# The last four rows of w4: a load written as 8 groups of 16 partitions instead of 128 partitions

## Chip, core and metric

One core of one Trainium2 chip. The metric is device time in microseconds (us) of one execution, taken as the median of several. A "packet" below is one entry of the DMA records: the move of one contiguous row by one of the core's 16 DMA engines. A "completion" is one entry of a semaphore's record of landings. A load of the kernel before has sixteen, which I read as one an engine: those of the last load come 0.3 to 0.4 us after an engine's last packet (the last packet of all ends at 209.82, the last completion is at 210.21). Both are in the trace with their times. No record names the DMA engine, so an engine is followed by its packets: in the kernel before, 99% start 3 or 4 ns before the recorded end of the one before, the others at most 24 ns before and 10 ns after it.

## The reference

Attention over a sliding window of a KV cache plus a small MLP, at batch 4 with one new token. Only the last line of the MLP matters here.

```python
xn = layernorm(x)                                   # x: [4, 1, 576] bf16
# A: q = xn @ wq; scores over the last 2048 rows of k_cache (16 heads); softmax; @ v_cache; @ wo
# B: x1 = xn + hs; hs is zero for one token, as its shifts move every value out
h2 = gelu(layernorm(x1) @ w3) @ w4                  # w3 [576, 4608], w4 [4608, 576]
return x + A(xn) + x1 + h2
```

(So w1 and w2 do not matter, and the kernel leaves them out.)

## The kernel before

Nearly all the time is the loading of 87 MB: K and V of 16 heads at 2 MB each, wq, wo, w3 and w4. SP (SyncE) issues all loads, in one order, w4 last. w4 is loaded in five pieces, so that the matrix engine can use one while the next arrives; the last piece is four rows per partition, 128 x 4608 B.

```python
    W4_PIECES = [0, NFH // 2, NFH, NFH + 9, NFH + 14, NF]      # NFH = 18, NF = 36: ..., 9, 5 and 4 rows

    def load_w4():
        t = wp.tile([P, NF, D], BF16, tag="w", name="w4_sb")   # P = 128 partitions, D = 576
        for lo, hi in zip(W4_PIECES, W4_PIECES[1:]):
            e = lo // NFH
            src = B_w4[e * (F // 2):(e + 1) * (F // 2), :].rearrange("(p i) n -> p i n", i=NFH)
            nc.sync.dma_start(out=t[:, lo:hi, :], in_=src[:, lo - e * NFH:hi - e * NFH, :])
        w_tiles["w4"] = t
    # ...
    def acc_matmuls(lhsT, rhs):                                # 4 matmuls for each row of w4
        for i in range(NQD):
            nc.tensor.matmul(out=acc[i * QD:i * QD + B, :], lhsT=lhsT, rhs=rhs[:, i * CW:(i + 1) * CW],
                             start=False, stop=False, skip_group_check=True)

    def mlp_out(lo, hi):
        w4 = w_tiles["w4"]
        for i in range(lo, hi):
            acc_matmuls(gT[:, i, :], w4[:, i, :])
    # ... attention, w3, gelu -> gT ...
    pieces = list(zip(W4_PIECES, W4_PIECES[1:]))
    mlp_out(*pieces[0])
    o_spread(hl)
    o_pick(hl)
    mlp_out(*pieces[1])
    o_proj(hl)
    for lo, hi in pieces[2:]:
        mlp_out(lo, hi)

    fin = const.tile([P, CW], out.dtype)
    nc.vector.tensor_copy(out=fin[:], in_=acc[:])              # then four small output DMAs
```

## Time and profile before

| | before |
|---|---|
| median time | 216.23 us (216.14 to 216.32, 3 runs) |
| span of the profiled run | 214.6 us |
| PE busy | 121.0 us, 56% |
| loads (queue q1) | 87.17 MB, 95.7% of 16 engines' span |

From the page of the kernel before. The DMA row gives the mean busy share of the 16 DMA engines in tenths, in 40 equal slices of the span; the GB/s row is what they moved. The q lines give packets, MB and the share of 16 engines' span.

```profile
span 214.6 us, 6449 instructions
PE 121.0 (56%) x2893; PEld 94.9 (44%) x2893; DVE 118.0 (55%) x223; ACT 70.1 (33%) x258; POOL 6.1 (3%) x14
...
DMA  5999999999999999999999999999999999999960
GB/s 207 429 437 434 428 429 425 425 425 437 426 429 423 437 431 419 439 425 434 431 428 425 428 428 430 422 434 431 429 418 428 437 419 425 437 427 422 419 262 12
...
q1 hardware_dynamic: 7080, 87.17, 95.7%
q8 instruction: 22, 0.36, 0.6%
```

The DMA engines are busy from the second slice to the last but two, and no compute engine is over 56%. The kernel is bound by its loads. Without moving fewer bytes, the place to look for a gain is the last two slices, where the rate falls from 419 to 262 to 12 GB/s.

The end of the chain of waits of the kernel before, read downwards: when each step began, how long it took, what it was.

```profile
152.04 30.72 DMA kn<-in_A_k_cache_dram
182.76 0.02 issue
182.78 27.43 DMA w_sb<-in_B_w_dram
210.21 0.04 issue
210.26 0.68 PE acc L247 x16
210.93 0.02 issue
210.96 0.31 DVE fin L480
```

The load of w4's last piece lands at 210.21; its 16 matmuls and a cast follow at once. What moves 210.21 moves the time.

The timeline of the kernel before, the lines of the last three pieces of w4 (36, 20 and 16 matmuls) and the cast: start, length, and in brackets the idle time before and what ended it.

```profile
207.14 0.73 PE L247 MATMUL acc<-w_sb,gT 128*4 128x144 bf16 x36 [1.17 <-DMA w_sb<-in_B_w_dram]
208.88 0.77 PE L247 MATMUL acc<-w_sb,gT 128*4 128x144 bf16 x20 [1.00 <-DMA w_sb<-in_B_w_dram]
210.26 0.65 PE L247 MATMUL acc<-w_sb,gT 128*4 128x144 bf16 x16 [0.61 <-DMA w_sb<-in_B_w_dram]
210.96 0.31 DVE L480 CAST fin<-acc 128x144 bf16<-128x144 f32 x1 [5.87 <-PE acc L247]
```

PE waits before each.

The sixteen completions of the last piece in the trace:

```
205.50 205.62 205.65 205.70 205.73 205.77 206.55 207.32 | 208.64 208.78 208.83 209.74 209.96 210.07 210.15 210.21
```

Six engines are done by 205.77, two more by 207.32 (I put them down to the five 8 KB instruction fetches of another queue, q14: around those at 154.0 and 163.6 us two completions go from 0.51 and 0.95 us behind the first, at the load of 151.44, to 1.11 and 1.93, at that of 166.02), and eight come from 208.64 on. The packets say why. PE's instructions are fetched by DMA too, in 16 KB blocks (the 22 packets of q8). The blocks fall on eight of the sixteen engines in a fixed rotation: an engine that carries the first carries the ninth and the seventeenth. Around one such block an engine's packets read (start in ns, length, bytes, queue):

```
31906  611 16384 q1
32513  929 16384 q8     <- instruction fetch
33428 1107 16384 q1
34531  612 16384 q1
```

From there on the engine is 1.415 us behind, for good. The completions of the earlier loads show it step by step. Before the first fetch the sixteen lie within 0.56 us of each other. After the fetch that starts at 15.0 us one engine is 1.58 us behind the first; each further fetch puts one more behind, until eight are. Then the second round begins: the ninth fetch (107.8) leaves one engine 2.91 us behind, the seventeenth (168.5) one 4.49 us. Two or three fetches in 210 us make the late eight up to 4.7 us later than the early six. No engine catches up: the sixteen of the last piece still lie 4.71 us apart.

### The profile page before, as it was taken

To read this page: it belongs to the slowest core of one execution; us is meant where nothing else is said; L and a number is where in the kernel's file an instruction comes from. 1 tells how busy PE (TensorE), PEld (TensorE's weight loads), DVE (VectorE), ACT (ScalarE), POOL (GpSimd) and SP (SyncE) were. 2 spreads that over 40 slices of the span, in tenths; PEclk is the share of its full clock that TensorE was granted. 3 is DMA by queue.
4 is the path that set the end of the run, shared out by engine and by line. 5 is a ranking of instruction groups with operands and counts; after the bars stand their busy time and mean duration, and the time that the engine had idled before them with its cause. 6 is when DMAs were issued, how large, how long until landed. Compare 5 with 4: busy or idle time off the path is not lost. (4 is left out here: it accounts for less than half of the span.)

```text
span 214.6 us, 6449 instructions
## 1 busy us (share of the span) xinstructions
PE 121.0 (56%) x2893; PEld 94.9 (44%) x2893; DVE 118.0 (55%) x223; ACT 70.1 (33%) x258; POOL 6.1 (3%) x14
## 2 busy tenths in 40 slices
PE   0461355647470017157999577677474705779752
PEld 0350143445360015145899456555453604557641
DVE  5608799766470047348610798785573924854210
ACT  0000005571634001607070045570725340709600
POOL 5400100000000000000000000000000000000000
PEclk9999999999999999999999999999999999999995
DMA  5999999999999999999999999999999999999960
GB/s 207 429 437 434 428 429 425 425 425 437 426 429 423 437 431 419 439 425 434 431 428 425 428 428 430 422 434 431 429 418 428 437 419 425 437 427 422 419 262 12
DMA packets 7123, 87.58 MB, mean 408 GB/s; under 512 B 820, under 2 KB 824, under 8 KB 1336
## 3 DMA queue, kind: packets, MB, share of 16 engines
q1 hardware_dynamic: 7080, 87.17, 95.7%
q8 instruction: 22, 0.36, 0.6%
q14 instruction: 5, 0.04, 0.0%
q10 hardware_dynamic: 16, 0.00, 0.0%
HBM read 87.17 MB, written 0.00 MB: 406 GB/s over the span
## 5 line engine op out<-in xcount | busy, mean ns | idle before, releaser
L302 ACT ACTIVATE pt<-S 32x128 bf16<-32x128 f32 x256 | 68.5, 268 | 92.0 <-issue 55.3
L259 DVE STREAM_TRANSPOSE kt<-kn 128x1024 int32<-128x1024 int32 x64 | 74.3, 1205 | 11.4 <-DMA kn<-in_A_k_cache_dram 11.4
L313 PE MATMUL O<-pt,vn 128*128 128x8 bf16 x1024 | 37.4, 169 | 43.2 <-DMA vn<-in_A_v_cache_dram 41.7
L313 PEld LDWEIGHTS <-vn 128*128 128x128 bf16 x1024 | 34.4, 105 | 51.3 <-DMA vn<-in_A_v_cache_dram 43.6
L273 PE MATMUL S<-qz,kt 128*128 128x32 bf16 x1024 | 39.1, 189 | 25.2 <-DVE kt L259 25.2
L273 PEld LDWEIGHTS <-kt 128*128 128x128 bf16 x1024 | 33.6, 106 | 36.1 <-DVE kt L259 30.4
L287 DVE TENSOR_REDUCE m<-mxT 8x1 f32<-8x128 f32 x16 | 4.4, 277 | 42.6 <-PE mxT L285 42.6
L316 PE MATMUL O<-pt,ones_bf 128*128 128x64 bf16 x128 | 17.1, 226 | 0.0
L302 ACT ACT_TABLE_LOAD x1 | 1.3, 1283 | 32.6 <-DVE mx L280 32.6
L368 PEld LDWEIGHTS <-w_sb 128*128 128x128 bf16 x144 | 11.4, 164 | 0.5 <-issue 0.4
L368 PE MATMUL AB<-ln2T,w_sb 128*128 128x4 bf16 x144 | 11.5, 202 | 0.0
L280 DVE TENSOR_REDUCE mx<-S 128x8 f32<-128x512 f32 x16 | 10.4, 652 | 1.0 <-PE S L273 1.0
L295 PE MATMUL S<-dg,ones_bf 8*128 8x512 bf16 x16 | 9.6, 601 | 0.1
L265 PE MATMUL S<-negbig,ohT 4*128 4x512 bf16 x16 | 9.6, 601 | 0.0
L316 PEld LDWEIGHTS <-ones_bf 128*128 128x128 bf16 x128 | 8.4, 104 | 0.0
L370 PE MATMUL AB<-ln2T,w_sb 128*128 128x4 bf16 x36 | 7.3, 202 | 0.0
L247 PE MATMUL acc<-w_sb,gT 128*4 128x144 bf16 x144 | 4.8, 294 | 2.8 <-DMA w_sb<-in_B_w_dram 2.8
L324 DVE TENSOR_REDUCE dn<-O 128x8 f32<-128x64 f32 x16 | 3.3, 208 | 5.5 <-PE O L316 5.5
L375 DVE COPY g_x<-AB 128x144 f32<-128x144 f32 x1 | 0.3, 307 | 10.7 <-PE AB L370 10.7
L285 PE MATMUL mxT<-ident_f,mx 128*8 128x128 f32 x16 | 6.0, 374 | 0.3 <-DVE mx L280 0.3
L370 PEld LDWEIGHTS <-w_sb 128*128 128x128 bf16 x36 | 5.9, 165 | 0.0
L247 PEld LDWEIGHTS <-gT 128*4 128x4 bf16 x144 | 3.4, 104 | 3.6 <-issue 3.5
(72 smaller groups left out, 64.9 us busy)
## 6 DMA issues: line engine op xcount, KB each, us to landing
kn<-in_A_k_cache_dram SPq DMA_DIRECT2D x16, 2048.0 KB, 29.3
vn<-in_A_v_cache_dram SPq DMA_DIRECT2D x16, 2048.0 KB, 27.0
wo_sb<-in_A_wo_dram SPq DMA_DIRECT2D x4, 1152.0 KB, 28.8
w_sb<-in_B_w_dram SPq DMA_DIRECT2D x2, 2304.0 KB, 31.8
wq_sb<-in_A_wq_dram SPq DMA_DIRECT2D x4, 1024.0 KB, 4.9
w_sb<-in_B_w_dram SPq DMA_DIRECT2D x3, 1296.0 KB, 32.8
w_sb<-in_B_w_dram SPq DMA_DIRECT2D x2, 576.0 KB, 32.2
w_sb<-in_B_w_dram SPq DMA_DIRECT2D x1, 720.0 KB
```

The lines of the kernel that those rows point to most:

```text
L247: nc.tensor.matmul(out=acc[i * QD:i * QD + B, :], lhsT=lhsT, rhs=rhs[:, i * CW:(i + 1) * CW], start=False, stop=False, skip_group_check=True)
L259: nc.vector.transpose(out=kt[:], in_=src)
L265: nc.tensor.matmul(out=S_ps[h][:].rearrange("p g k j -> p (g k) j"), lhsT=ohT[:], rhs=nb, start=True, stop=False, skip_group_check=True)
L273: nc.tensor.matmul(out=S_ps[h][:, s * (SC // NQD) + g].rearrange("p k j -> p (k j)"), lhsT=kt[:, ib, g * NQD:(g + 1) * NQD, e:2 * QD:2].re ...
L280: nc.vector.reduce_max(out=mx[:], in_=S_ps[h][:].rearrange("p g k j -> p j (g k)"), axis=AX.X)
L285: nc.tensor.transpose(out=mxT[:], in_=st[h][:], identity=ident_f[:])
L295: nc.tensor.matmul(out=S_ps[h][:].rearrange("p g k j -> p (g k) j"), lhsT=ones_bf[0:NJ, :], rhs=dg, start=False, stop=False, skip_group_ch ...
L302: nc.scalar.activation(out=PT[h][kb * QD:(kb + 1) * QD, :, c4, :], in_=S_ps[h][c4 * QD:(c4 + 1) * QD, :, kb, :], func=ACT.Exp, scale=scale)
L313: nc.tensor.matmul(out=O_ps[h][:, 0:NJ], lhsT=vn[:, g * NQD + s, :], rhs=pt[:, g, s, :], start=(g == 0 and s == 0), stop=False, skip_group ...
L316: nc.tensor.matmul(out=O_ps[h][:, NJ:].rearrange("p (c j) -> p c j", j=NJ), lhsT=ones_bf[:], rhs=pt[:, g:g + DG, s, :], start=False, stop= ...
L368: nc.tensor.matmul(out=g_ps[:, i, :], lhsT=w3[:, j * F + e * (F // 2) + f0:j * F + (e + 1) * (F // 2):NFH], rhs=ln2T[:, j, :], start=False ...
L370: nc.tensor.matmul(out=g_ps[:, i, :], lhsT=w3[:, KJ * F + f0:KJ * F + F // 2:NFH], rhs=ln2T[:, KJ + e, :], start=False, stop=False, skip_g ...
```

## The change

The last piece keeps its bytes and its place in the queue. Its source is written as 8 groups of 16 partitions, so that, as I read its purpose, the transfer is split over 8 DMA engines with 16 packets each and no longer over 16 with 8 each. If those eight are the early ones, the late ones have nothing more to do for this piece and end sooner.

```diff
             src = B_w4[e * (F // 2):(e + 1) * (F // 2), :].rearrange("(p i) n -> p i n", i=NFH)
-            nc.sync.dma_start(out=t[:, lo:hi, :], in_=src[:, lo - e * NFH:hi - e * NFH, :])
+            src = src[:, lo - e * NFH:hi - e * NFH, :]
+            if hi == NF:
+                src = src.rearrange("(u p) i n -> u p (i n)", u=8)
+            nc.sync.dma_start(out=t[:, lo:hi, :].rearrange("p i n -> p (i n)") if hi == NF else t[:, lo:hi, :], in_=src)
```

## The prediction

> **What bounds it now.** The loads. In the 40-slice view the DMA row reads 9 from the second slice to the last but one; the SP queue moves 87.17 MB, 95.7% of 16 engines' span (queue table). The chain of waits ends with a DMA of w4 (27.43 us from 182.78), the last 16 matmuls at 210.26 and the cast at 210.96; the span ends at 214.6. PE waits for the last three w4 pieces (1.17, 1.00, 0.61 us in the timeline).
>
> The 16 engines do not end together. The sixteen completions of the last piece come at 205.50 to 205.76 (six), 206.55, 207.32, and then eight from 208.64 to 210.21. The packets of the trace, each starting as the one before it on its engine ends, show why: the 22 instruction fetches of 16 KB (queue q8) go in turn to eight of the engines, and each sets its engine back by 1.415 us.
>
> **What the change does.** Same bytes, same queue order, same compute instructions. The last piece (128 rows of 4608 B, 178 ns a packet) goes from 16 engines x 8 packets (1.40 us) to 8 engines x 16 packets (2.80 us). [...] No record of this run names an engine. [...]
>
> **Worth, three cases (estimates from those durations).**
> 1. Only the engines limit. The late eight end 1.40 us sooner (last completion 210.21 to 208.85); the early ones end at 206.6 to 208.4. PE then runs the last 20 and 16 matmuls (0.77 and 0.65 us) together after 208.9: 0.8 us saved, 215.4 us.
> 2. The SBUF side limits. [...] A packet here moves at 27.3 GB/s beyond a fixed 9 ns[...]. [...] the end stays near 210.2, or 0.5 us later [...]: 216.2 to 216.8 us.
> 3. The eight are the late ones: +1.4 us or more, 217.6 us and above.
>
> I weigh 2 highest, then 1, then 3.
>
> **Prediction: 216.2 us, 8 in 10 between 215.1 and 217.6. Faster by over 2%: 0.01; within 2%: 0.96; slower by over 2%: 0.03.**
>
> **What would show it.** The 4608 B packets of the last piece on eight engines, 16 each. Case 1: they stay at 178 ns, no wait or a short one between the last two w4 pieces, last matmul near 210.1. Case 2: they take 200 to 400 ns, and so do packets of the late engines at that time. Case 3: completions of the last piece come from late engines only, until 211.6 or later. Nothing before 203 us changes.
>
> **What would make it wrong.** Fetches falling elsewhere at the end; packets split differently[...].

The "8 engines x 16 packets" is my assumption, and so is case 1's, that the eight are early ones; the low weight of case 3 rested on it. The sums: 215.4 us in case 1; in case 2 the end stays near 210.2 (216.2 us) or comes 0.5 us later (216.8 at most); 217.6 us and above in case 3; together 216.2 us. The 27.3 GB/s and 9 ns of case 2 fit the usual packets of the kernel before: 4096 B in 159 ns, 4608 B in 178, 10368 B in 389, 16384 B in 611, 18432 B in 686.

## More of the kernel before

Unless said otherwise every run quoted is a fast one.

The windows view of the kernel before (stretch, its length, busy us and instruction counts of PE, PEld, DVE, ACT and POOL, granted PE clock, DMA share, GB/s):

```profile
204.00:206.00 2.00, 1.98 (x75) 1.57 (x72) 0.85 (x2) 0.00 (x0) 0.00 (x0) 1.00 0.85 354
206.00:208.00 2.00, 0.73 (x36) 0.58 (x36) 0.00 (x0) 0.00 (x0) 0.00 (x0) 1.00 0.54 224
208.00:210.00 2.00, 0.77 (x20) 0.56 (x20) 0.00 (x0) 0.00 (x0) 0.00 (x0) 0.69 0.29 116
```

From 206 to 210 us about half, then under a third, of the DMA engines work. They do not end together.

## The result, and the profile after

| | before | after |
|---|---|---|
| median time | 216.25 us (216.14 to 216.32, 4 runs) | 216.28 us (216.14 to 216.39, 4 runs) |
| ratio | | 1.0004, 95% interval 0.9989 to 1.0019 |
| span of the profiled run | 214.6 us | 214.6 us |
| last completion of w4 | 210.21 | 210.22 |
| completions of the last piece | 16 | 16 |
| its packets | 128 of 4608 B, 178 ns each | 128 of 4608 B, 178 ns each |

A ratio is the mean time of one kernel's fast runs over the mean of the other's in the same rounds, so it is not quite the ratio of the medians quoted. All outputs are right.

The page of the kernel after:

```profile
span 214.6 us, 6449 instructions
...
DMA  5999999999999999999999999999999999999960
...
q1 hardware_dynamic: 7080, 87.17, 95.7%
```

Its chain of waits, the end:

```profile
183.01 27.20 DMA w_sb<-in_B_w_dram
210.22 0.04 issue
210.26 0.68 PE acc L250 x16
...
210.96 0.31 DVE fin L483
```

Its timeline, the same four groups:

```profile
207.15 0.73 PE L250 MATMUL acc<-w_sb,gT 128*4 128x144 bf16 x36 [0.83 <-DMA w_sb<-in_B_w_dram]
208.89 0.49 PE L250 MATMUL acc<-w_sb,gT 128*4 128x144 bf16 x20 [1.01 <-DMA w_sb<-in_B_w_dram]
210.26 0.65 PE L250 MATMUL acc<-w_sb,gT 128*4 128x144 bf16 x16 [0.89 <-DMA w_sb<-in_B_w_dram]
210.96 0.31 DVE L483 CAST fin<-acc 128x144 bf16<-128x144 f32 x1 [5.82 <-PE acc L250]
```

And its windows:

```profile
206.00:208.00 2.00, 1.05 (x53) 0.69 (x42) 0.00 (x0) 0.00 (x0) 0.00 (x0) 1.00 0.55 224
208.00:210.00 2.00, 0.49 (x20) 0.33 (x20) 0.00 (x0) 0.00 (x0) 0.00 (x0) 0.85 0.26 105
```

The last 16 matmuls and the cast start at the same hundredth of a microsecond, and the DMA engines thin out in the same way. The sixteen completions, 205.44 to 210.22, show no trace of a split over eight engines.

The built program settles it: the DMA is the same one. A source written as 8 groups (16 partition rows apart) of 16 (one partition row apart) describes the same walk as 128 partitions one row apart. The builder folds the two dimensions into one, and in both kernels the instruction carries (step and count, in elements):

```
source       [10368 x 128] [1 x 2304]     offset 1335168
destination  [20736 x 128] [1 x 2304]     offset 18432
```

It carries 128 on both sides, and in both kernels the load has sixteen completions and 128 packets of 178 ns. That the two are one DMA was to be seen without a run: the listing of the built instructions names the transfer 128x2304 before and after. I had that listing and did not look at that line.

### The profile page after: what moved, and what is told of

Same layout as the page of the kernel before. It is cut to its first block, busy times and chain, and to the rows that moved or that the text cites. A ratio compares the mean times of both kernels' runs of the same rounds, so it can differ in the third digit from the quotient of the medians.

```text
span 214.6 us, 6449 instructions
## 1 busy us (share of the span) xinstructions
PE 120.9 (56%) x2893; PEld 95.0 (44%) x2893; DVE 118.1 (55%) x223; ACT 70.3 (33%) x258; POOL 6.2 (3%) x14
```

## The experiments

The kernel after answers nothing about eight engines, because it never used them. So the experiments first make the intended split real, then ask why it does what it does. A transfer whose dimensions cannot be folded must put the rows on other partitions, and so the matching rows of gT must be permuted (one matmul with a permutation matrix and two copies, before the loads end). Runs of one group shared a chip and its runs of the kernel before.

My first theory was the prediction's middle case: the writing into the on-chip memory limits, so that moving packets to other engines gains nothing. The rivals were its other two cases: only the engines limit (a gain), or the eight chosen are the late ones (a loss). Which partitions and engines would collide was my assumption, which no run here shows. Theory B below is that the writing limits as well, theory C that the engines used are the late ones.

### e0_perm_only: the permutation alone

```diff
         nc.vector.tensor_tensor(out=gT[:], in0=u[:], in1=xs[:], op=ALU.mult)
+        pm = const.tile([P, P], BF16, name="pm")
+        nc.vector.tensor_copy(out=pm[:], in_=ident_bf[:])        # here the identity
+        gp = ps_m.tile([P, 4, B], F32, tag="m", name="gp")
+        nc.tensor.matmul(out=gp[:].rearrange("p i b -> p (i b)"), lhsT=pm[:],
+                         rhs=gT[:, NF - 4:NF, :].rearrange("p i b -> p (i b)"), start=True, stop=True)
+        nc.vector.tensor_copy(out=gT[:, NF - 4:NF, :], in_=gp[:])
```

> Control: the load of before, plus the small extra step that the next three kernels need (a 128x128 permutation matrix, here the identity, one matmul and two copies after the gelu). Every theory expects the time of before, 216.25 us within 0.1%, the last w4 piece on 16 engines with 8 packets of 178 ns, last completion near 210.2 us.

Measured: 216.30 us against 216.37, ratio 0.9995 (0.9979 to 1.0012), last completion 210.15. The added work costs nothing, so what e1 to e3 show is the load's doing.

### e1_eight: the split over eight engines, made real

```diff
+            if hi == NF:
+                src = src.rearrange("(p u) i n -> u p (i n)", u=8)      # 8 x 16, row order changed
+                dst = dst.rearrange("p i n -> p (i n)")                 # dst was t[:, lo:hi, :]
     # cut: the DMA itself; pm as in e0, but it permutes gT's rows to match
```

The source is now [10368 x 8] [82944 x 16] [1 x 2304], which cannot be folded.

> The change made real: the row order of the last four rows is such that the two outer dimensions (8 and 16) cannot be merged into 128, so that eight engines carry 16 packets each. Theory A (the change as written was folded back into the same 128-row transfer, and only the engines limit): packets stay at 178 ns, all on the eight early engines, last completion 208.85 us, some 0.8 us faster, 215.4 us. Theory B [...]: about half of the 4608 B packets take 200 to 530 ns, last completion 210.2 to 210.7 us, 216.2 to 216.8 us. Theory C [...]: completions on late engines only, 211.6 us or later, 217.6 us and more.

Measured: 219.86 us (219.06 to 220.54) against 216.37, ratio 1.0158 (1.0126 to 1.0190). There are eight completions:

```
208.82 209.11 209.16 209.43 210.79 212.01 213.91 214.42
```

So this is the split that the prediction had reckoned with, and it costs 3.5 us. The timeline of e1:

```profile
208.94 1.25 PE L252 MATMUL acc<-w_sb,gT 128*4 128x144 bf16 x36 [2.53 <-DMA w_sb<-in_B_w_dram]
211.85 0.77 PE L252 MATMUL acc<-w_sb,gT 128*4 128x144 bf16 x20 [1.66 <-DMA w_sb<-in_B_w_dram]
214.46 0.65 PE L252 MATMUL acc<-w_sb,gT 128*4 128x144 bf16 x16 [1.84 <-DMA w_sb<-in_B_w_dram]
```

All three groups are late, also the two whose pieces were not changed: by 1.8, 3.0 and 4.2 us against before. The windows of e1:

```profile
204.00:206.00 2.00, 2.00 (x72) 1.86 (x75) 0.84 (x2) 0.00 (x0) 0.00 (x0) 1.00 0.95 251
206.00:208.00 2.00, 0.41 (x16) 0.20 (x5) 0.00 (x0) 0.00 (x0) 0.00 (x0) 1.00 0.84 208
```

From 204 to 206 us the engines are busier than before (0.95 against 0.85) and move less (251 against 354 GB/s). The engines are not short of work; each packet takes longer. In the packet records the 4608 B packets have a median of 271.5 ns and a maximum of 549, where they took 178 before, and 5760 B packets of the piece before it go up to 645 (at most 227 before).

### e2_sixteen: sixteen engines, eight packets each, but other partitions

The same edit with u=16. Sixteen completions and 128 packets are those of before. What differs is how the transfer walks: each step of its outer dimension covers eight neighbouring partitions and, since the row order changes, reads every sixteenth of the 128 groups of rows. No record shows which engine takes which step. The expectation says that only the place of writing differs; that is not quite so. Its first forecast is for engines alone, the second for the theory that the writing limits.

> Same unmergeable form with 16 x 8 in place of 8 x 16: 16 engines, 8 packets each[...]. Only the place of writing differs from before. Engines alone: 178 ns a packet, last completion 210.2, 216.25 us. [...] about 40% of the 4608 B packets over 200 ns, last completion 1 to 1.3 us later, 217.3 us.

Measured: 218.54 us against 216.37, ratio 1.0099 (1.0084 to 1.0114); sixteen completions, the last at 212.44. A quarter of the 4608 B packets took 303 ns or more, up to 533. From the windows of e2:

```profile
204.00:206.00 2.00, 2.00 (x71) 1.76 (x69) 0.84 (x2) 0.00 (x0) 0.00 (x0) 1.00 1.05 250
```

The engines are full and the rate is 250 GB/s, as in e1. The transfer has as many completions and packets as before, so a shortage of engines cannot be the cause. The place of writing may be, but the changed reads of e2 are a rival that e2 alone does not exclude; e4 and e5 below, whose reads are the same, settle that the place of writing counts. I expected about 217.3 and got 218.5, so the direction is that of the theory that the writing limits, and the expected size was too small.

### e3_own_ports: eight engines, low partitions first

Four DMAs of 32 partitions each, 8 x 4, one behind the other, so that each of the eight engines first writes eight packets to partitions 0 to 63, then eight to 64 to 127 (four in each DMA, from its 32 packets and eight completions).

```diff
+            for q in range(4):
+                nc.sync.dma_start(out=t[32 * q:32 * q + 32, lo:hi, :].rearrange("p i n -> p (i n)"),
+                                  in_=src[32 * q:32 * q + 32].rearrange("(v u) i n -> u v (i n)", u=8))
```

> Eight engines as in e1_eight, but as four transfers of 32 partitions, 8 x 4[...]. Engines alone: 178 ns a packet, last completion 208.85, 215.4 us. [...] packets to partitions 0 to 63 take 178 ns, those to 64 to 127 up to 356 ns while the late engines are still at work, and the last completion stays at 210.2, 216.2 us.

Measured: 218.12 us against 216.37, ratio 1.0078 (1.0061 to 1.0095); the theory that the writing limits (the second forecast) had expected 216.2, a miss. The eight completions of the first and of the last of the four DMAs:

```
first  204.75 204.76 204.83 204.86 206.62 207.66 210.51 210.67
last   207.88 208.10 208.26 208.33 209.88 210.64 212.58 212.74
```

Two things follow. First, the eight engines used are six early ones and two late ones (210.51 and 210.67 in the first DMA, 2.85 us after the sixth); two early engines carry none of it. My prediction took all eight for early. The two late ones now have sixteen packets to do at the very end, alone and as fast as in the kernel before (178 ns each, in one of them from 209.50 to 212.30).

Second, a meeting is there in the packets. The early engines write their eight packets to partitions 0 to 63 at 178 ns; as soon as they turn to partitions 64 to 127, while late engines still write earlier pieces, theirs take about 355 ns, and the late engines' packets go from 389 to about 805 ns (10368 B) and from 220 to about 450 (5760 B). Both sides take about twice as long.

The last completion, 212.74, is 2.53 us later than before. Eight extra packets at 178 ns are 1.42 us of it; the remaining 1.1 us agrees with the earlier pieces of those engines ending late (their packets end at 209.33 and 209.49, where they ended near 208.3 before).

### e4_four_low and e5_four_high: the same work on two sets of partitions

This pair holds everything still but the partitions written; the rows read are the same too. The last 256 rows of w4 go to 32 partitions, in two DMAs of 4 x 4 partitions: partitions 0 to 15 and 32 to 47 in e4, 64 to 79 and 96 to 111 in e5. I take them to use four engines, the same in both (8 packets of 9216 B an engine in all), as 8 x 4 gave eight completions in e3; no record names them. In e3 packets to partitions 0 to 63 kept their 178 ns, those to 64 to 127 took about 355.

```diff
+    W4_PIECES = [0, NFH // 2, NFH, NFH + 9, NFH + 14, NFH + NE]          # NE = 16
+    def load_tail():                                                     # TB = 0 in e4, 64 in e5
+        kvt = kvp.tile([P, NC, Dh], BF16, tag="kv", name="tail_sb")
+        # ... viewed as [128, 8, 576], partitions TB to TB+48 set to 0
+        src = B_w4[F - TR:F, :].rearrange("(h v u i) n -> h u v (i n)", h=2, v=4, u=4)
+        for h in range(2):
+            nc.sync.dma_start(out=tail_sb[TB + 32 * h:TB + 32 * h + 16, :, :].rearrange("p i n -> p (i n)"), in_=src[h])
     # cut: load_tail() ahead of the last piece; gelu for the other row order; 32 matmuls over 48 partitions
```

> The last 256 rows of w4 go to 32 partitions only, 0 to 15 and 32 to 47, by two transfers of 4 x 4 partitions (4 engines, 4 packets of 9216 B each); the other engines carry 8 packets of 2304 B less per row pair. [...] Theory B [...]: nothing collides, 347 ns a packet, the late engines end 0.7 us sooner, last completion about 209.5, and only 8 matmuls after it: 215.3 us. [...]

> As e4_four_low in every instruction [...], but partitions 64 to 79 and 96 to 111 in place of 0 to 15 and 32 to 47. Engines alone: the same time as e4_four_low, 215.3 us, 347 ns a packet. [...] packets of the four engines take up to 700 ns and packets of four late engines double meanwhile; [...] last completion 211.5 to 212.5, 217.5 to 218.5 us.

(The first gave 217 us should the four engines not be early ones.)

Measured: e4 217.33 us against 216.15, ratio 1.0058 (1.0045 to 1.0071); e5 221.20, ratio 1.0234 (1.0220 to 1.0248). Both are slower than expected (215.3, and 217.5 to 218.5 if the writing limits). The 9216 B packets of these rows took 347 to 364 ns in e4, and a median of 687 in e5. One stretch of the windows of e4:

```profile
206.00:208.00 2.00, 2.00 (x74) 1.86 (x71) 0.84 (x2) 0.00 (x0) 0.00 (x0) 1.00 0.75 315
```

and of e5:

```profile
206.00:208.00 2.00, 2.00 (x68) 1.75 (x68) 0.84 (x2) 0.00 (x0) 0.00 (x0) 1.00 0.75 202
```

The same share of busy engines, 0.75, moves 315 GB/s in one and 202 in the other. The same bytes in the same packets are 3.9 us dearer when they go to partitions 64 to 79 and 96 to 111. The two kernels differ in nothing but the partitions written, so the place of writing is the cause. What is shared there was not shown.

But e4 lost where I had hoped for a gain. Its tail is clean, so the loss is earlier: the third piece of w4 already begins to land at 203.72, where before it was 202.37. The new constants had moved every tile behind them by 64 B against a multiple of 256 (a tile that began at byte 38144 of a partition now began at 38720), and 16 KB packets took a mean of 617.3 ns where they had taken 613.3.

### e8_shift64 and e6_four_low_aligned: that shift alone, and e4 without it

```diff
+    const.tile([P, 32], BF16, name="pad")        # e8: the kernel before, and 64 B of nothing
```

```diff
+    const.tile([P, 96], BF16, name="pad")        # e6: e4, and 192 B that restore the multiple of 256
```

> The kernel before with 64 unused bytes a partition, which moves every loaded tile by 64 bytes modulo 256 and changes nothing else. If place modulo 256 matters: a 16 KB packet takes 613 ns and 617 on average, the last completion comes 1.3 us later, 217.5 us. If not: 216.2 us.

> e4_four_low with 192 unused bytes a partition, so that every loaded tile starts at a multiple of 256 bytes in its partition again (in e4_four_low, and in e5, the new constants had moved them all by 64 bytes modulo 256, and a 16 KB packet took 613 ns and 617 on average in place of 611 and 613). If that shift explains why e4 was behind by 1.35 us before its tail began: packets back at 611 ns, third piece of w4 lands as in before, and the time is e4 less 1.35 us, 216.0 us. If not: as e4, 217.3 us.

Measured: e8 218.00 us against 216.34, ratio 1.0079 (1.0066 to 1.0092), 16 KB packets at a mean of 617.2 ns; e6 215.97 (215.72 to 216.46), ratio 0.9991 (0.9978 to 1.0004), 16 KB packets back to a mean of 613.6. So 64 unused bytes cost 1.7 us. Each engine moves 5.45 MB, or 333 packets of 16 KB; at 3.9 ns more each, that is, by estimate, 1.3 of the 1.8 us by which the last load lands later. The rest is in the late engines: the first completion of the last piece is 1.43 us later (206.93), the last 1.80 (212.01). The 16 KB fetches of q8 took a mean of 1065 ns where they had taken 935, and three of them on one engine make 0.39 us (an estimate from these means). Why they took longer was not tested.

In e6 the last completion is at 209.54, 0.67 us before that of the kernel before, and yet the cast starts at 210.90 (before: 210.96). From the 5-row piece on PE has 60 matmuls to do, where it had 36. The gain goes into them and into a stop of 0.26 us that the next two runs show larger.

### e7_four_low_early and e9_tail_first: those matmuls moved earlier

e7 is e6 with the small DMAs issued ahead of the last three pieces and their matmuls after the third piece; e9 puts these matmuls ahead of the third piece.

```diff
-    for lo, hi in pieces[2:]:
+    for k in range(NT):                                          # e9; in e7 after mlp_out(*pieces[2])
+        acc_matmuls(gt2[TB:TB + 48, k, :], w_tiles["tail"][TB:TB + 48, k, :])
+    for lo, hi in pieces[2:]:
         mlp_out(lo, hi)
```

> e6 with the two transfers to partitions 0 to 15 and 32 to 47 issued ahead of the last three pieces of w4 in place of behind the second last, and their 32 matmuls ahead of those pieces' last 28. The late engines end some 0.7 us sooner than in before, as in e6, but after their last completion (about 209.5) only 8 matmuls are left: 215.3 us. If the four early engines become the last instead, they end near 209 and the time is the same or 0.3 us more.

> e7 with the 32 matmuls on the 32-partition rows put ahead of the third piece of w4 as well: their data land near 203.8 us and PE waits about 0.8 us for the third piece there. In e6 and e7 the last completion was 0.67 and 0.66 us sooner than in before (about 209.55), but PE had 60 to 96 matmuls left. Here only the 9-, 5- and 2-row pieces are left, each as it lands: the last 8 matmuls end near 210.0 in place of 210.9, 215.4 us, 0.4% faster than before. If PE is still behind: 216.0.

Measured: e7 216.20 us against 216.34, ratio 0.9989 (0.9975 to 1.0002); e9 216.04 against 216.15, ratio 0.9985 (0.9969 to 1.0001). Both are misses. The profile of e9 shows a new wait, in its chain:

```profile
207.22 0.48 PE acc L266 x19
207.71 2.09 issue
209.79 1.61 PE acc L266 x34
```

PE stands still for 2.09 us and waits for no data ("issue": for nothing that the profile shows). The same in the timelines of e6 (first line) and e7:

```profile
209.59 0.23 PE L266 MATMUL acc<-w_sb,gT 128*4 128x144 bf16 x4 [0.26 <-issue]
209.47 0.76 PE L266 MATMUL acc<-tail_sb,gt 48*4 48x144 bf16 x17 [0.50 <-issue]
```

In the records of q8, a fetch of PE's instructions starts at 207.46 and lands at 208.35; PE goes on 1.44 us after that. In e7 the stop ends 1.35 us after a fetch landed; in e6 1.50 us after. Counted from the start of the program, the stop comes after 2904, 2903 and 2903 matmuls in e6, e7 and e9, although it falls into three different pieces of data. The kernel before ends with its 2893rd. I read the stop as PE out of instructions, which no record says outright: late in the kernel its matmuls come so thick (80 from 204 to 206 us in e9) that it runs through a block before the next (0.89 us in its fetch, from 207.46 to 208.35) has come.

### e11_shifted_stream: the block boundary moved

If so, moving the boundaries of the instruction blocks against the work should move or end the stop. e11 is e9 with 64 small matmuls without use (128 PE instructions) at the start of the kernel, where PE is idle.

```diff
+    for _ in range(64):
+        nc.tensor.matmul(out=AB[0:B, 480:480 + B], lhsT=ones_bf[:, 0:B], rhs=ones_bf[:, 0:B],
+                         start=False, stop=False, skip_group_check=True)
```

> e9 with 64 small matmuls (128 PE instructions) more at the start, where PE waits for the first weights, so that what PE runs at the end stands 128 instructions further on in its stream. In e9's profile PE stood still for 2.09 us from 207.70 us, in the middle of matmuls whose data had landed, with no releaser on record; two of e9's six runs (215.24, 215.41 us) were 0.7 us quicker than the other four. If that stop belongs to a place in the instruction stream (the arrival of a block of instructions), it moves some 128 instructions earlier, to a stretch where PE has time to spare, and the time is 215.3 us in all runs. If it belongs to something else, it stays: 216.0 us in most runs.

Measured: 214.86 us (214.75 to 214.99, 5 runs) against 216.12, ratio 0.9941 (0.9927 to 0.9954). It beats the kernel before by 0.6%, and so the kernel after, which took the same time. The timeline of e11:

```profile
205.18 0.81 PE L270 MATMUL acc<-wo_sb,op 128*4 128x144 bf16 x20
206.20 0.48 PE L270 MATMUL acc<-wo_sb,op 128*4 128x144 bf16 x12 [0.20 <-issue]
...
209.00 0.48 PE L270 MATMUL acc<-w_sb,gT 128*4 128x144 bf16 x20 [1.01 <-DMA w_sb<-in_B_w_dram]
209.69 0.30 PE L270 MATMUL acc<-w_sb,gT 128*4 128x144 bf16 x8 [0.20 <-DMA w_sb<-in_B_w_dram]
210.03 0.31 DVE L518 CAST fin<-acc 128x144 bf16<-128x144 f32 x1 [5.05 <-PE acc L270]
```

The stop is now 0.20 us and lies ahead of the third piece; the fetch behind it landed 1.57 us before PE went on. It again comes after 2904 matmuls from the start, the 64 new ones among them. So it belongs to a place in PE's instructions and not to a piece of data, as the expectation had it; that the block arrives late there, rather than something else tied to that place, rests on the fetch times. After the last load only 8 matmuls are left. The cast is 0.93 us earlier than before. The spans differ by 1.5 us (213.1 against 214.6): the other 0.6 us are in the closing waits, from the start of the output to the end of the span (2.7 us where they were 3.28), as in e6 and e9. All three have two further DMAs; whether these are the reason was not tested. A control with only the 64 matmuls and the load of before was prepared and not run, as the number of runs was used up: how much of the gain the shift alone gives stays open.

### e10_more_pe: more instruction fetches

If the fetches set the late engines back, more of them should set them back more. e10 is the kernel before with 512 small matmuls spread over the heads.

```diff
                                  start=False, stop=False, skip_group_check=True)   # the scores' matmuls
+            for _ in range(2):
+                nc.tensor.matmul(out=AB[0:B, 480:480 + B], lhsT=ones_bf[:, 0:B], rhs=ones_bf[:, 0:B],
+                                 start=False, stop=False, skip_group_check=True)
```

> The kernel before with 512 small matmuls more, spread evenly over the 64 score stages, on data at hand, into an unused corner: 1024 PE instructions more, so 4 instruction fetches of 16 KB more, nothing else. If fetches make the late engines late: 26 fetches in all, two of the eight engines get a fourth one, each sets its engine back by 1.4 us, and the last completion comes up to 1.4 us later, 217.5 us (216.9 to 217.9), although PE has idle time to spare. If lateness has another cause: 216.3 us.

Measured: 230.48 us against 216.15, ratio 1.0669 (1.0654 to 1.0684), with 26 fetches where there were 22. But the matmuls cost far more than their fetches. From the waits of SP, the loads' issuer (us in total, times, longest):

```profile
SPq L107 <- PE O L319: 104.3, 12, 15.2
```

SP held back loads for PE, whose busy time rose from 121.0 to 175.4 us; PE became the limit. From about 137 us on the queue of loads ran dry now and then, and the completions of the last piece drew together, to a spread of 1.86 us from 4.71. That fits lateness being carried along only while the queue of loads does not run dry. As a test by time e10 is inconclusive. Up to 137 us, though, it answers: its ninth fetch starts at 97.7 us (before: 107.8), and of the load that begins to land at 99.96 us one engine is already 3.23 us behind the first. In the kernel before, no engine is more than 1.83 us behind at that load (100.03); the first at this level comes two loads later, 2.91 us behind (109.77). The engines fall behind when the fetches come, sooner where these come sooner.

## Why the prediction was right or wrong

The time was right, 216.2 predicted and 216.28 measured, within 2% as given 0.96. The reason was not: the number held because nothing had changed. That is luck. With the split made real (e1) the time was 219.86 us, outside the range given.

- **What bounds the kernel: right.** Loads to the end, engines ending apart, a w4 DMA last in the chain. "Nothing before 203 us changes" held too, and would have held for any reason.
- **The step that failed: "The last piece (128 rows of 4608 B, 178 ns a packet) goes from 16 engines x 8 packets (1.40 us) to 8 engines x 16 packets (2.80 us)."** It did not: 16 completions, the same DMA in the program. I took the number of engines from the dimensions in the source text, 8 and 16, and not from those the instruction carries, 128. "Packets split differently" stood among what would make the prediction wrong, but without a check that could have been made.
- **That the eight engines used would all be early ones, as case 1 has it: wrong.** In e3 they are six early and two late.
- **Case 1, only the engines limit, 215.4 us: refuted** by e1 to e3, all slower, and by e4 against e5.
- **Case 2, the memory side limits: that the place of writing counts is shown, what is shared there is not** (e5 against e4: only the partitions written differ, 3.9 us; e3: packets doubled, on both sides; e2: the same sixteen completions and number of packets, another order of partitions and reads, 1% slower). Its size, "216.2 to 216.8 us", was wrong for the intended split: e1 took 219.86. The term missed is delay to the pieces ahead: packets of both sides slow down (178 to about 355 ns and 389 to about 805 in e3), and the earlier pieces of the late engines hold up PE (by 1.8 and 3.0 us in e1).
- **Case 3, the eight are the late ones: partly so**, two of eight, worth 1.42 us at the end of e3.
- **The late engines by instruction fetches: right.** 1.415 us a fetch, eight engines in rotation; one engine more falls behind after each fetch, and in e10, up to 137 us, sooner as the fetches come sooner. The time of e10 itself says nothing about it.

## What to carry to other kernels

A rearranged access pattern may be folded back into the same DMA, as here (8 x 16 in order: sixteen completions, as before; out of order, in e1: eight): read the shape in the built instruction, or count the completions, before reasoning about engines. When DMA engines end apart, work moved to the early ones need not pay: here it slowed their packets and those of the late ones where it was written to partitions 64 to 127 (178 to about 355 ns and 389 to about 805 in e3), and the same work cost 3.9 us more there than on low partitions (e5 against e4). A busy share that rises while GB/s falls was the sign of it (0.95 and 251 GB/s in e1, 0.85 and 354 before). A transfer that lands earlier is worth only what the compute behind it can use, and its order and its instruction fetches decide that (in e6, e7 and e9 the last load landed 0.6 to 0.7 us sooner and the time did not move beyond the noise; e11 gained 1.3 us, some 0.6 of it in the closing waits).
